# Early weight chunks, u products among output products and transpositions, and other memory for the first channel weights

## The chip, the core and the metric

The kernel runs on one core of a Trainium2 chip. The core has five engines with a queue of instructions each: TensorE (PE, with its weight loads shown as PEld), VectorE (DVE), ScalarE (ACT), GpSimd (POOL) and SyncE (SP), which here issues most of the transfers (DMA). The metric is the device time of one execution in microseconds (us); lower is better.

## The reference

Four steps are computed in turn, for 4 batches of 576 tokens with 512 features, in float32:

```
scores = 1/sqrt(D) * rot(q) @ rot(k).T ; attn = softmax(scores) ; x = heads(attn @ v)
h = gelu(x @ w_in) ; u, v = h[..., :512], h[..., 512:]
v_n = (v - mean) / sqrt(var + 1e-06) * g_ln
x = x + (u * (w_sg @ v_n + b_sg)) @ w_out           # over the tokens: w_sg is 576 x 576
u = x + (x.T @ U @ V).T                             # rank 32, over the tokens
out = u + relu(u @ w_ch1) @ w_ch2                   # 512 -> 2048 -> 512
```

All weights of the last three steps arrive as 64-bit words and are turned into float32 on the chip.

## The kernel before

**Stages.** The attention runs until about 305 us, then the gated stage for batches 0 to 3 until about 555 us, then the channel stage to the end. A float32 product is made of three products of halves (high x high, high x low, low x high); a tile's name ends in H or h for its high part and in L or l for its low part. High parts are copied by ACT, low parts are differences, made by POOL or DVE (`less`).

**The gated stage.** For a batch b it consists of these steps, each a group of products on PE and what other engines make of it:

- `v_step`: products v; gelu on ACT; the normalisation on DVE and ACT into VH, VL and, for the last 64 tokens, VT (L648, L651).
- `u_step`: products u; gelu on ACT into the tile ug.
- `s_step`: spatial products m of the matrices WSH/WSL with VH, VL (and VT); then on DVE g (L672, L673), which reads m and ug, on ACT its high part, on POOL its low part. LAST_G is the last step of g.
- `o_step`: output products w; DVE adds them to X (L691).
- `y_step`: transpositions t of X on PE (L710); ACT copies them to YH (L712), DVE makes YL (L718); of the last 64 tokens DVE makes the low part in a piece of YH (L714).
- `z_step`: products z of 512 columns from YH and YL (L728); from them ACT and DVE make Z (L731, L732).
- `h_step`: products q of V and Z; DVE adds them to X (L740). The four of a batch are q_0 to q_3.

**Weights on the side.** `other_weights` converts the four blocks of w_out, each by one ACT step (L85) and four DVE steps (L86 to L89) from a block loaded into a YH or YL tile. `first_weights` converts the first 26 blocks ("chunks", numbered from 0) of w_ch1 and w_ch2, each by an ACT step (L775) and four DVE steps (L771 to L774) out of a tile `raw` into a tile `cb`; every second chunk ends with a combine, four more DVE steps (L782 to L785), and a store of cb to memory off the core (COMBO). A generator gives out one chunk at each call of `chunk()`. A chunk's steps may be issued only behind the last marked step of DVE and the last gelu of the program so far (`issue_after` with LAST_D); a weight of w_out stands behind the last g in the same way.

**What sets the order.** In the attention and the channel stage all engines' orders are written by hand. In the gated stage only PE's is: it runs the products as the code lists them. For ACT, DVE, POOL and SP a scheduler puts the steps into an order, within what the data and `issue_after` allow. The calls for batch b are mixed with those for n = b + 1: spatial products of b, v products of n, output products of b, then u products of n among the transpositions, z and q of b.

**The channel stage.** `channel` has 12 periods of 14 ticks, each with the seven products r (L907) of w_ch1 and the seven products a of w_ch2 in a Strassen-like scheme; the operands of the second group are r1h, r1l to r7h, r7l (copies on ACT L828, differences L831). Step lists with times in ticks set every engine's order. In period 0 the high parts of the next group's weights are loaded from COMBO into YH and YL tiles (`loads`), copied by ACT to w1h, w2h (`highs`), and the low parts just used (w1l, w2l, "lows") are stored. Batch 3's transpositions, z, Z and q run in this period's first ticks. The tiles W1, W2, ROP, cb3 (`spare`) and `words` are opened in the memory that the gated stage leaves, in the order of the code.

## Time and profile before

| what | value |
|---|---|
| time, median of 3 runs (lowest to highest) | 925.42 us (924.62 to 926.44) |
| profiled execution: its own time | 929.44 us |
| its span | 927.6 us |
| mean granted clock of PE, share of full speed | 0.982 |
| busy PE, PEld | 894.3 us (96%), 809.0 us (87%) |
| busy DVE | 746.0 us (80%) |
| busy ACT, POOL | 465.3 us (50%), 400.9 us (43%) |

PE is nearly always busy over the span, so a gain has to come out of its few gaps, or out of stretches at a lower granted clock. The shares are means over three stages that differ: which engine holds PE up has to be read stage by stage.

### The profile page before, as it was taken

To read this page: it belongs to the slowest core of one execution; us is meant where nothing else is said; L and a number is where in the kernel's file an instruction comes from. 1 tells how busy PE (TensorE), PEld (TensorE's weight loads), DVE (VectorE), ACT (ScalarE), POOL (GpSimd) and SP (SyncE) were. 2 spreads that over 40 slices of the span, in tenths; PEclk is the share of its full clock that TensorE was granted. 3 is DMA by queue.
4 is the path that set the end of the run, shared out by engine and by line. 5 is a ranking of instruction groups with operands and counts; after the bars stand their busy time and mean duration, and the time that the engine had idled before them with its cause. 6 is when DMAs were issued, how large, how long until landed. Compare 5 with 4: busy or idle time off the path is not lost.

```text
span 927.6 us, 14333 instructions
## 1 busy us (share of the span) xinstructions
PE 894.3 (96%) x5279; PEld 809.0 (87%) x5279; DVE 746.0 (80%) x991; ACT 465.3 (50%) x719; POOL 400.9 (43%) x302
## 2 busy tenths in 40 slices
PE   8999999999999998798999987999999999999998
PEld 4677788878877998797899986999999999999997
DVE  6666888898998497799798886889788877897557
ACT  4555666666666554423524436455455555544232
POOL 6995787777736575142244314341011111041010
PEclk9999999999999999799899999999999999999999
DMA  6787777687662412435235238669479568737721
GB/s 189 204 183 174 208 195 192 164 214 180 164 170 57 144 46 70 145 126 192 87 124 194 87 136 275 240 230 376 166 268 353 215 213 284 249 123 266 277 98 69
DMA packets 101331, 170.36 MB, mean 184 GB/s; under 512 B 32823, under 2 KB 50509, under 8 KB 101261
## 3 DMA queue, kind: packets, MB, share of 16 engines
q1 hardware_dynamic: 100960, 169.36, 59.1%
q8 instruction: 42, 0.69, 0.3%
q14 instruction: 29, 0.23, 0.1%
q10 hardware_dynamic: 300, 0.08, 0.0%
HBM read 110.07 MB, written 41.49 MB: 163 GB/s over the span
## 4 chain that ended last, share of the span: by engine, by line
PE 62%; DVE 20%; DMA 5%; issue 4%; POOL 4%; ACT 4%; SPq 0%; DVEq 0%; POOLq 0%; ACTq 0%
PE pv L278 12%; PE st L251 7%; PE sm L209 3%; PE u L588 2%; DVE cb L774 2%; DVE cb L773 2%; DVE cb L771 1%; DVE g L672 1%; DVE g L673 1%; DVE cb L782 1%; DVE cb L772 1%; DMA YL<-combo 1%; PE a0X L907 1%; DVE MX L214 1%; PE w L588 1%
## 5 line engine op out<-in xcount | busy, mean ns | idle before, releaser
L214 DVE TENSOR_REDUCE MX<-sm 128x1 f32<-128x576 f32 (+1 forms) x160 | 117.0, 747 | 38.4 <-PE sm L209 31.9
L278 PE MATMUL pv<-pc,VV 128*65 128x288 f32 (+1 forms) x516 | 146.7, 408 | 0.0
L251 PE MATMUL st<-Q,K 65*128 65x288 f32 (+3 forms) x640 | 126.9, 321 | 3.5 <-DMA Q<-mt 2.1
L251 PEld LDWEIGHTS st<-Q,K 65*128 65x128 f32 (+3 forms) x640 | 95.6, 179 | 18.3 <-DMA Q<-mt 2.3
L254 ACT ACTIVATE pc<-st 128x576 f32<-128x576 f32 x129 | 83.1, 645 | 33.2 <-PE st L251 30.7
L278 PEld LDWEIGHTS pv<-pc,VV 128*65 128x65 f32 (+1 forms) x516 | 69.7, 137 | 29.4 <-issue 0.7
L831 POOL TENSOR_TENSOR r1l<-t,r1h 128x768 fp32r<-128x768 f32 x12 | 22.6, 1884 | 157.3 <-ACT r1h L828 141.4
L831 POOL TENSOR_TENSOR r7l<-tmp,r7h 128x768 fp32r<-128x768 f32 x12 | 25.6, 2129 | 120.4 <-ACT r7h L828 89.3
L209 PE MATMUL sm<-K,Q 128*128 128x288 f32 (+1 forms) x320 | 72.4, 316 | 1.7 <-ACT pc L254 0.6
L173 POOL TENSOR_TENSOR Q<-raw,Q 128x576 fp32r<-128x576 f32 x30 | 45.7, 1522 | 31.8 <-ACT Q L168 31.7
L209 PEld LDWEIGHTS sm<-K,Q 128*128 128x128 f32 (+1 forms) x320 | 50.4, 179 | 7.7 <-DVE MX L214 1.3
L154 POOL TENSOR_TENSOR raw<-raw,tab 128x576 f32<-128x576 f32 x31 | 50.5, 1630 | 2.5 <-DMA raw<-in_qk 2.5
L331 DVE TENSOR_TENSOR X<-stage,rb 64x576 f32<-64x576 f32 x30 | 47.5, 1586 | 1.4 <-DMA rb<-rr 1.0
L588 PE MATMUL u<-XH,setA 128*128 128x288 f32 x256 | 46.7, 299 | 1.4 <-DVE X L691 1.4
L156 POOL TENSOR_TENSOR raw<-raw 128x576 f32<-128x576 f32 x31 | 47.6, 1537 | 0.6
L155 POOL TENSOR_TENSOR raw<-raw,tab 128x576 f32<-128x576 f32 x31 | 44.4, 1431 | 0.0
L588 PEld LDWEIGHTS u<-XH,setA 128*128 128x128 f32 x256 | 38.8, 191 | 2.0 <-DVE X L691 1.7
L541 POOL TENSOR_TENSOR GL<-g,GH 128x576 fp32r<-128x576 f32 x16 | 26.4, 1653 | 32.7 <-ACT GH L674 32.7
L588 PE MATMUL v<-setA,XH 128*128 128x512 f32 x128 | 39.6, 390 | 0.0
L432 POOL TENSOR_TENSOR XL<-X,XH 128x576 fp32r<-128x576 f32 x16 | 27.1, 1715 | 23.7 <-ACT XH L429 23.7
L775 ACT ACTIVATE cb<-raw 128x512 f32<-128x512 f32 x26 | 17.5, 672 | 39.4 <-DMA raw<-in_w 27.8
L294 ACT ACTIVATE stage<-pv 65x576 f32<-65x576 f32 x31 | 20.0, 647 | 29.6 <-PE pv L278 29.6
(1149 smaller groups left out, 2508.4 us busy)
## 6 DMA issues: line engine op xcount, KB each, us to landing
raw<-in_qk SPq DMA_DIRECT2D x31, 576.0 KB
combo<-cb SPq DMA_DIRECT2D x16, 896.0 KB
YH<-combo SPq DMA_DIRECT2D x27, 512.0 KB
raw<-in_w SPq DMA_DIRECT2D x26, 512.0 KB
K<-Q SPq DMA_DIRECT2D x30, 288.0 KB
YL<-combo SPq DMA_DIRECT2D x15, 512.0 KB
u<-setA SPq DMA_DIRECT2D x16, 384.0 KB
w2l<-lows SPq DMA_DIRECT2D x12, 512.0 KB
```

Source lines behind the costliest of these rows:

```text
L154: lambda: e.tensor_tensor(raw[:, 0], raw[:, 0], tab[:, 0], ALU.mult),
L155: lambda: e.tensor_tensor(raw[:, 1], raw[:, 1], tab[:, 1], ALU.mult),
L156: lambda: e.tensor_tensor(raw[:, 0], raw[:, 0], raw[:, 1], ALU.add),
L173: nc.gpsimd.tensor_tensor(Q2[:, :S], rot, f(Q1), ALU.subtract)
L209: nc.tensor.matmul(ps[:TS[t], n, :HALF], Q1[:, t * P:t * P + TS[t]], K1[:, n * HALF:(n + 1) * HALF], start=True, stop=True)
L214: nc.vector.tensor_reduce(MXs[h % 2][:TS[t], t:t + 1], ps[:TS[t], :, :HALF], AX.XY, ALU.max)
L251: nc.tensor.matmul(ps[:kk, n, :HALF], l[:, c * P:c * P + kk], r[:, ns], start=st, stop=not st)
L254: nc.scalar.activation(h2(pc[:kk]), ps[:kk, :, :HALF], AF.Exp, scale=0.125)
L278: nc.tensor.matmul(o, l, r, start=(c == 0 and j == 0), stop=(c == NC - 1 and j == len(pr) - 1))
L331: nc.vector.tensor_tensor(X[b][rows, pr], STAGE.pop(h - 1 + a)[:D], RB[i][:, a], ALU.mult)
L588: nc.tensor.matmul(o, l, rr, start=(first and j == 0), stop=(last and j == n - 1))
L831: return e.tensor_tensor(out, a, b, ALU.subtract)
```

## The change

The code changes in six places.

- In batch 0 the gelu of the v products goes to a YL tile instead of a raw tile.
- `first_weights` is opened right behind `x_tail(0)`, and chunks 0 and 1 are called behind u_1 and u_3 of batch 0, ahead of its first spatial products. The other chunks are called at other places: for n = 1 seven as before, for n = 2 and n = 3 nine each, and chunk 25 behind m_0 of batch 3 instead of m_1.
- PE's order for n = 1: u_0 and u_1 stand ahead of the transpositions, u_2 between these and z, u_3 between z and its last product; the q products move behind the spatial products m_0 and m_1 of batch 1.
- PE's order for n = 2: u_0 stands between the transpositions and z.
- cb3 and words are opened after W1, W2 and ROP. By the addresses they now lie in the memory of the spatial weights WSH and WSL; before, they lay in memory that the output products read.
- In period 0 of the channel stage the stores of lows that stood at ticks 3.6 and 8.0 are at 6.7, and the times of the high copies change.

```diff
@@ -625,7 +625,7 @@
         nt = last - first + 1
         slot[0] = 1024 - slot[0]
         hv = ug.rearrange("p a b -> p (a b)")[:, slot[0]:slot[0] + 1024].rearrange("p (a b) -> p a b", a=2)
-        hv = (hv if b else raw_tile())[:, :nt]
+        hv = (hv if b else py.tile([P, 2, DF], F32, tag="YL", name="YL", bufs=2))[:, :nt]
         gelu(hv, ps[:pp, :nt])
         st = p2.tile([P, 2, 6], F32, tag="bst", name="bst", bufs=2)
         mv = p2.tile([P, 2, 2], F32, tag="bmv", name="bmv", bufs=2)
@@ -869,11 +869,11 @@
 
         def spare_tile():
             return pr.tile([P, 7, HF], F32, tag="cb3", name="cb3", bufs=1).rearrange("p a b -> p (a b)")
-        spare, word = {0: spare_tile()}, [word_tile()]
         seta = [t.rearrange("p a b -> p (a b)")[:, 4 * TB:] for t in SETA]
         W1 = [p3.tile([P, 5, FG], F32R, name=f"w1{x}") for x in "hl"]
         W2 = [p3.tile([P, 7, FG], F32R, name=f"w2{x}") for x in "hl"]
         ROP = {n: [pr.tile([P, 2, TB], F32R, name=f"r{n}{x}") for x in "hl"] for n in range(1, 8)}
+        spare, word = {0: spare_tile()}, [word_tile()]
 
         def wslot(c, x, j, n=1):
             if c == 0 and j >= 5:
@@ -1019,11 +1019,11 @@
                     at(o + t, lambda n=n, y=y: nc.sync.dma_start(UKEPT[p][n][:, y], f(UOP[n][y])))
             if g not in [x for _, x in ORDER[:i]] and g < NG - 1:
                 for c, j in KEPT:
-                    at(o + (0.05 if c == 0 and j < 2 else 3.6 if c == 0 else 8.0 if i == 0 else 6.0), lambda c=c, j=j: nc.sync.dma_start(LOWS[c][g][:, j], f(wslot(c, 1, j))))
+                    at(o + (0.05 if c == 0 and j < 2 else 6.7 if i == 0 else 3.6 if c == 0 else 6.0), lambda c=c, j=j: nc.sync.dma_start(LOWS[c][g][:, j], f(wslot(c, 1, j))))
             if h != g:
                 fresh = h not in [x for _, x in ORDER[:i]]
                 loads = (2.3, 4.0, 4.5, 6.5, 6.6) if i == 0 else (0.2, 0.3, 1.3, 2.4, 5.0) if i > 3 else (1.4, 1.8, 3.2, 3.5, 5.0)
-                highs = (3.85, 5.45, 6.5, 9.0, 9.4) if i == 0 else (3.85, 4.75, 6.0, 7.0, 9.4) if i == 1 else (4.1, 4.75, 6.0, 7.0, 9.4)
+                highs = (4.1, 6.2, 7.0, 9.0, 9.4) if i == 0 else (3.85, 4.75, 6.0, 7.0, 9.4) if i == 1 else (4.1, 4.75, 6.0, 7.0, 9.4)
                 tops = (15.1, 16.2) if fresh else (13.2, 14.2)
                 seconds = (11.65, 13.0, 13.6) if fresh or i == 3 else (6.1, 7.1, 8.1)
                 for c, j0, j1, load, t, lo, e in (
@@ -1114,6 +1114,9 @@
 
     spatial_weights()
     x_tail(0)
+    fw = first_weights()
+    next(fw)
+    chunk = lambda: next(fw, None)
     for t in range(NC):
         v_step(0, t)
     RB[NP - 1] = p2.tile([P, S], F32, tag="g", name="g", bufs=2)
@@ -1122,15 +1125,14 @@
             fn()
     for k0 in range(KT):
         u_step(0, k0)
+        if k0 % 2:
+            chunk()
     ow = other_weights()
     with ExitStack() as es:
         for x in LASTS:
             es.enter_context(tc.issue_after(x.ins))
         next(ow)
         x_split(1)
-    fw = first_weights()
-    next(fw)
-    chunk = lambda: next(fw, None)
     for b in range(B - 1):
         n = b + 1
         for d in range(KT):
@@ -1141,7 +1143,12 @@
                 with ExitStack() as es:
                     es.enter_context(tc.issue_after(LAST_G[0].ins))
                     next(ow, None)
-            elif d % 2:
+            if b == 1:
+                if d < 2:
+                    run(h_step, b - 1, 2 * d, 2 * d + 1)
+                if d % 2:
+                    chunk()
+            if b == 2 and d % 2 == 0:
                 chunk()
         run(v_step, n, 0, 1)
         chunk()
@@ -1162,34 +1169,41 @@
             v_step(n, 2)
             chunk()
             run(v_step, n, 3, 4)
+            if n == 3:
+                chunk()
+        if n == 1:
+            u_step(n, 0)
             chunk()
-        us = iter(range(KT))
-        if n < B - 1:
-            if n % 2:
-                u_step(n, next(us))
+            u_step(n, 1)
             run(y_step, b, 0, 2)
-            if n % 2:
-                chunk()
+            u_step(n, 2)
             run(z_step, b, *range(NC - 1))
             y_step(b, 4)
-            u_step(n, next(us))
+            u_step(n, 3)
+            z_step(b, 4)
             chunk()
+        elif n == 2:
+            run(y_step, b, 0, 2)
+            u_step(n, 0)
+            chunk()
+            run(z_step, b, *range(NC - 1))
+            y_step(b, 4)
+            u_step(n, 1)
             z_step(b, 4)
-            u_step(n, next(us))
+            u_step(n, 2)
+            chunk()
             run(h_step, b, 0, 1)
-            u_step(n, next(us))
-            chunk()
+            u_step(n, 3)
             run(h_step, b, 2, 3)
-            run(u_step, n, *us)
         else:
-            for k0 in us:
+            for k0 in range(KT):
                 u_step(n, k0)
                 if k0 % 2:
                     chunk()
     a, b = B - 2, B - 1
     for d in range(KT):
         s_step(b, d)
-        if d == 1:
+        if d == 0:
             chunk()
         if d < 2:
             y_step(a, 2 * d)
```

What this moves on the engines is not seen in the diff alone. In the rows below a number in a product's name only counts tiles; 128x512 and so on is a step's shape.

DVE at the first spatial products of batch 0, before; m_0 and m_1 are the products that g waits for, L86 to L89 the weights of w_out:

```order
L648 TENSOR_TENSOR VH<-raw,VH 64x512
L651 TENSOR_TENSOR VT<-raw,VT 64x512
L86 TENSOR_SCALAR cb<-cb 128x512
L87 TENSOR_SCALAR cb<-cb 128x512
L88 SCALAR_TENSOR_TENSOR cb<-YH,cb 128x512
L89 SCALAR_TENSOR_TENSOR cb<-YH,cb 128x512
L672 SCALAR_TENSOR_TENSOR g<-m_0_3621,small,bh 128x576
L673 TENSOR_TENSOR g<-g,ug 128x576
```

DVE at the same place after the change, from VT on; L771 to L774 are chunks, L782 is the first step of a combine:

```order
L651 TENSOR_TENSOR VT<-YL,VT 64x512
L771 TENSOR_SCALAR cb<-cb 128x2x256
L86 TENSOR_SCALAR cb<-cb 128x512
...
L774 SCALAR_TENSOR_TENSOR cb<-raw,cb 128x2x256
L89 SCALAR_TENSOR_TENSOR cb<-YH,cb 128x512
L771 TENSOR_SCALAR cb<-cb 128x2x256
L772 TENSOR_SCALAR cb<-cb 128x2x256
L773 SCALAR_TENSOR_TENSOR cb<-raw,cb 128x2x256
L774 SCALAR_TENSOR_TENSOR cb<-raw,cb 128x2x256
L672 SCALAR_TENSOR_TENSOR g<-m_0_3641,small,bh 128x576
L782 TENSOR_TENSOR cb<-cb 128x256
L673 TENSOR_TENSOR g<-g,ug 128x576
```

Chunks 0 and 1 and the first combine, twelve steps, now stand between VT and the end of the first g's; the scheduler didn't place any of them ahead of VT.

PE from the transpositions of batch 0 to the last z, before, with what stands of one u product shortened:

```order
L588 MATMUL u_0_4017<-XH,setA_71 128x288 x2
L710 MATMUL t_0_4043<-ident,X 128x128 x8
L710 MATMUL t_2_4056<-ident,X 128x128 x8
L728 MATMUL z_4077<-YH,U_76 128x512
...
L710 MATMUL z_4077<-ident,X 64x128 x4
L588 MATMUL u_1_4093<-XH,setA_70 128x288 x2
...
L588 MATMUL q_0_4161<-V_77,Z_4132 128x288 x2
L588 MATMUL q_1_4165<-V_77,Z_4132 128x288 x2
L588 MATMUL u_3_4169<-XH,setA_70 128x288 x2
```

PE after the change, from the same transpositions to the first q products:

```order
L588 MATMUL u_1_4071<-XH,setA_71 128x288 x2
L710 MATMUL t_0_4097<-ident,X 128x128 x8
L710 MATMUL t_2_4110<-ident,X 128x128 x8
L588 MATMUL u_2_4123<-XH,setA_70 128x288 x2
...
L728 MATMUL z_4149<-YH,U_76 128x512
...
L588 MATMUL m_0_4207<-WST,VT 128x288 x4
L588 MATMUL q_0_4241<-V_77,Z_4192 128x288 x2
L588 MATMUL q_1_4245<-V_77,Z_4192 128x288 x2
L588 MATMUL m_1_4257<-WS,VH 128x288 x4
```

A u product now stands between the transpositions and z, and the q products stand behind the first spatial product of batch 1. On DVE the step that they wait for, L732, stood behind one step of the next chunk; it now stands behind three:

```order
L714 TENSOR_TENSOR YH<-z_4149,YH 64x512
L771 TENSOR_SCALAR cb<-cb 128x512
L772 TENSOR_SCALAR cb<-cb 128x512
L773 SCALAR_TENSOR_TENSOR cb<-raw,cb 128x512
L732 TENSOR_TENSOR Z_4192<-z_4149,Z_4192 32x512
L774 SCALAR_TENSOR_TENSOR cb<-raw,cb 128x512
L672 SCALAR_TENSOR_TENSOR g<-m_0_4207,small,bh 128x576
L740 TENSOR_TENSOR X<-q_0_4241,X 128x576
```

The first q sum (L740) moved behind a g of batch 1.

ACT at the start of the channel stage, before; z, Z are batch 3's, r0x and r0z are sums of products r:

```order
L828 ACTIVATE r1h<-t_5853 128x768
L828 ACTIVATE w1h<-YH 128x1024
L731 ACTIVATE Z_5888<-z_5791 128x512
L828 ACTIVATE tmp<-r0z 128x768
L828 ACTIVATE w2h<-words 128x512
L828 ACTIVATE w1h<-YL 128x1024
L828 ACTIVATE r3h<-tmp 128x768
L828 ACTIVATE w1h<-YH 128x512
```

ACT at the same place after the change:

```order
L828 ACTIVATE r1h<-t_5853 128x768
L731 ACTIVATE Z_5882<-z_5791 128x512
L828 ACTIVATE tmp<-r0z 128x768
L828 ACTIVATE w1h<-YH 128x1024
L828 ACTIVATE w2h<-words 128x512
L828 ACTIVATE r3h<-tmp 128x768
L828 ACTIVATE w1h<-YL 128x1024
L828 ACTIVATE w1h<-YH 128x512
```

Z and the copy of r0z moved ahead of the first high copy, and r3h ahead of the one out of YL.

## Rows read from the trace of the kernel before

**Rows 1.** Waits of PE, 310 to 600 us: us in total, times, longest

```profile
PE t L710 <- DVE X L691: 4.1, 1, 4.1
PE z L728 <- DVE YL L718: 4.1, 4, 2.6
PE a0X L907 <- DVE X L740: 3.7, 1, 3.7
PE z L728 <- DVE YH L714: 2.1, 1, 2.1
...
PE r0x L907 <- ACT tmp L828: 1.4, 2, 1.1
```

**Rows 2.** Busy PE, PEld, DVE, ACT, POOL by stretch; granted clock, DMA share, GB/s

```profile
325.70:340.60 14.90, 14.90 (x115) 14.90 (x114) 13.78 (x14) 8.60 (x15) 11.48 (x8) 1.00 0.22 71
340.60:351.50 10.90, 10.90 (x50) 9.01 (x49) 10.76 (x13) 2.69 (x4) 6.01 (x4) 1.00 0.00 0
364.40:382.90 18.50, 10.96 (x54) 8.91 (x53) 16.26 (x30) 6.40 (x9) 3.50 (x3) 0.72 0.55 184
```

**Rows 3.** Timeline of DVE, 326 to 353: start, duration, line, output<-inputs

```profile
332.24 1.65 DVE L86 TENSOR_SCALAR cb<-cb 128x512 f32<-128x512 f32 x1
...
351.49 0.75 DVE L673 TENSOR_TENSOR g<-g,ug 128x576 f32<-128x576 f32 x1
```

**Rows 4.** Timeline of POOL, 313 to 412; in brackets the idle time before and its releaser

```profile
329.78 5.39 POOL L432 TENSOR_TENSOR XL<-X,XH 128x576 fp32r<-128x576 f32 x3 [3.42 <-ACT XH L429]
...
391.81 6.17 POOL L432 TENSOR_TENSOR XL<-X,XH 128x576 fp32r<-128x576 f32 x4 [6.28 <-ACT XH L429]
```

**Rows 5.** Timeline of DVE, 374 to 392

```profile
375.98 0.42 DVE L785 TENSOR_TENSOR cb<-cb 128x256 f32<-128x256 f32 x1
378.04 2.35 DVE L718 TENSOR_TENSOR YL<-t,YH 128x1024 fp32r<-128x1024 f32 x2 [1.63 <-ACT YH L712]
380.31 0.42 DVE L771 TENSOR_SCALAR cb<-cb 128x512 f32<-128x512 f32 x1
...
381.23 0.69 DVE L773 SCALAR_TENSOR_TENSOR cb<-raw,cb 128x512 uint32<-128x512 uint32 x1
```

**Rows 6.** Timeline of PE, 310 to 420, from u to the spatial products of batch 1

```profile
365.90 0.53 PE L588 MATMUL u<-XH,setA 128*128 128x288 f32 x2 [1.44 <-DVE X L691]
...
374.15 2.40 PE L710 MATMUL t<-ident,X 128*128 128x128 f32 x10 [4.13 <-DVE X L691]
378.06 0.80 PE L728 MATMUL z<-YH,U 128*128 128x512 f32 x1 [1.51 <-ACT YH L712]
...
393.24 0.69 PE L588 MATMUL q<-V,Z 128*128 128x288 f32 x4
393.77 0.69 PE L588 MATMUL m<-WS,VH 128*128 128x288 f32 x4
```

**Rows 7.** Timeline of PE and of DVE, 436 to 462, batch 1

```profile
437.66 0.50 PE L728 MATMUL z<-YH,U 128*128 128x512 f32 x1 [0.49 <-ACT YH L712]
440.76 0.79 PE L728 MATMUL z<-YL,U 128*128 128x512 f32 x1 [2.60 <-DVE YL L718]
...
442.28 1.23 DVE L718 TENSOR_TENSOR YL<-t,YH 128x1024 fp32r<-128x1024 f32 x1 [1.51 <-ACT YH L712]
...
460.78 0.69 PE L588 MATMUL m<-WS,VH 128*128 128x288 f32 x4
```

**Rows 8.** Timeline of all engines, 569 to 586, start of the channel stage

```profile
571.79 0.95 DVE L970 TENSOR_TENSOR tmp<-r0x,tmp 128x768 f32<-128x768 f32 x1
...
575.33 1.06 ACT L828 ACTIVATE w1h<-YL 128x1024 fp32r<-128x1024 f32 x1 [5.18 <-DMA YL<-combo]
576.29 0.83 ACT L828 ACTIVATE r3h<-tmp 128x768 fp32r<-128x768 f32 x1
...
584.06 0.95 DVE L831 TENSOR_TENSOR r6l<-tmp,r6h 128x768 fp32r<-128x768 f32 x1
...
585.41 0.51 PE L907 MATMUL a0X<-r6h,w2h 128*128 128x384 f32 x2
```

## The prediction

> **What bounds the kernel now.** I read the waits of PE first. Between 310 and 600 us PE stands idle in a few places only [rows 1]: 4.1 us for a transposition that needs X, 4.1 us in four spatial-low products z that need YL, 3.7 us ahead of a0X, 2.1 us for one z that needs YH, 1.4 us for r0x, and 1.44 us for a product u [rows 6]. Everywhere else in that stretch PE runs without a gap. So the change can gain only in those places, and the next question is who keeps PE waiting there. The busy time by stage answers it for batch 0 [rows 2]: while PE makes the spatial products m (325.7 to 340.6) DVE is busy 13.78 of 14.90 us, in the next products v 10.76 of 10.90, and around the transpositions (364.4 to 382.9) 16.26 of 18.50 while PE works 10.96. DVE is the bound of batch 0, and PE's waits there are what DVE's queue leaves over. The timeline of DVE says why the queue is long [rows 3]: a step of a kind that takes 0.42 us alone [rows 5] takes 1.65 us at 332.24, while POOL runs the differences XL [rows 4]. Last I read the start of the channel stage [rows 8].
>
> **Part 1, two chunks ahead of the first spatial products.** A chunk is four DVE steps; alone two take 0.42 and two 0.69 us, together 2.22 [rows 5]; every second chunk ends in a combine of four steps of 0.42, 1.7 us [rows 5]. DVE is idle for long before 326, but the chunks don't get there: the code lets a chunk's steps out only behind the last marked DVE step, which is VT's (L651), and the order shows them right behind it, ahead of the first g. From there DVE was full. Ahead of the last YL of batch 0 stood four chunks before, now seven (0 to 6). Three chunks and one combine are 3 x 2.22 + 1.7 = 8.4 us. One ACT step more ahead of VH and VT adds 0.6. The 1.63 us that DVE waited for YH before its two YL [rows 5] is filled by chunk 6, so 8.4 + 0.6 - 1.6 = 7.4 us: YL, which ended at 378.04 + 2.35 = 380.4, ends at 387.8.
>
> The contention needs a choice. A step that meets POOL ends about when POOL's operation ends (1.65 us for 0.42 us of work [rows 3, 5]), so it loses some 1.2 us. POOL has 12 operations in the two stretches [rows 2], as many after the change, and they already found DVE steps to hold up. I take no further loss, since the number of POOL operations doesn't change; the ends are 5 us more (four or five more meetings) and 4.7 us less (the idle DVE time of 351 to 383 takes some of it in).
>
> The Trainium skill (SBUF — State Buffer, Who interferes with whom) says that a DVE instruction with two SBUF inputs, or in a two-port mode, and a GpSimd instruction lock each other out, and that the second one waits for the whole of the first. Taken alone it would have each of the 12 early steps wait for an operation of its own; by the rows only POOL's operations are counted, not DVE's. By the one the time is 931.9, by the other 918.3; the first is the slower rival.
>
> **Part 2, u products between output products and transpositions.** In batch 0 PE now runs u_0, u_1, t_0, t_2, u_2, z, u_3. A matmul of 288 columns takes 0.133 us (four in the 0.53 from 393.24 to 393.77 [rows 6]), a u product of 24 so 3.2, two q products of eight in all 1.07. That puts 6.4 us of work where PE waited 1.44, 4.13 and 1.51 us [rows 6], and would hide all of it, and the half clock with it (0.72 granted there [rows 2]), if DVE stood still. DVE is 7.4 us later, though, so PE now waits earlier: v's first product for the place of m_0 until g is read, the third and fourth output product for gelu of v. Behind YL's end PE has four z products of 512 columns (at the same rate 0.94 us), four transpositions (0.5, ten took 2.40 at half clock [rows 6]), u_3 (3.2) and the last z (0.24): 4.9 us, so the next spatial products start at 387.8 + 4.9 = 392.7, against 393.77 before [rows 6], when two q products (1.07) were done already. Term A: -1.0 + 1.1 = **+0.1 us**, ends -4.6 and +5.
>
> **Part 3, q products behind m_0 and m_1.** They now need Z in the middle of PE's stream. DVE's Z stands behind three steps of chunk 7; that chunk's first ACT step stands behind gelu of u_3, which ends at 387.8 + 0.94 + 0.5 + 3.2 + 0.7 = 393.1, so the three can start at 393.7. POOL makes four XL meanwhile, 1.54 us each; before, they began 2.0 us ahead of m_0 (391.81 [rows 4], 393.77 [rows 6]), now so at 390.7, and last to 396.9. The three steps end about with the second, third and fourth XL [rows 3], 397.5, and Z, as long as such a step, at 398.2. PE has m_0 (28 matmuls, 3.7) done at 392.7 + 3.7 = 396.4: a new wait. Term B: **+1.8 us**, ends 0 (no contention: 393.7 + 1.5 + 0.7 lies before 396.4) and 2.6.
>
> In batch 1 u_0 moves in front of the z products. There the first z stood at 437.66, behind the transpositions, and a later one waited 2.60 us [rows 7]. PE comes 1.9 us late (A and B): 439.6, plus u_0 442.8. YL ended at 442.28 + 1.23 = 443.5 [rows 7]; ahead of it now stands one combine more (1.7) and some of the lateness (0.4): 445.6. Four z (0.94) and the transpositions (0.5) end at 447.0; u_1 to u_3, z and q are 9.6 + 0.24 + 1.07 = 10.9, so the spatial products of batch 2 start at 457.9, against 460.78 [rows 7]: 2.9 early, from 1.9 late. Term C: **-4.8 us**, ends -3 and -6.5.
>
> By the end of batch 1 both kernels have done 16 chunks. In batch 2 and 3 PE had no wait but the z for YH (2.1 us [rows 1]); there I take DVE as 2.1 us early, since its last combine ahead of g is now done sooner but its q sums later, while PE is 2.9 early, so the wait grows. Chunk 25 moves from behind m_1 to behind m_0, with as much work ahead of that YH as before. Term D: **+0.8 us**, ends -0.9 and +0.9.
>
> **Part 4, first weights.** The buffers cb3 and words now lie in WS, last read by m, not in memory that the output products read to the end; their loads can start some 14 us earlier. PE's first channel product waited little for them, so this alone gives little: it moves ACT and DVE steps forward that PE's short waits there hang on (r0x for copies on ACT, 1.4 us in two [rows 1]). I take 1.1 of that. The new times do more. Before, a load into YL was issued behind five stores of lows, ACT waited 5.18 us for it, and r3h, which needs nothing of it, stood behind on ACT until 576.29 [rows 8]. Its input was done at 571.79 + 0.95 = 572.74. Now r3h stands ahead of that step and the stores behind the loads: r3h 3.5 us earlier, and with it r3l, X, a0X. PE then meets DVE again: r6l began at 584.06 and now begins at 580.6, ends 581.5, and the second a0X product, at 585.41 before [rows 8], can start then: 3.9 us. Term E: -3.9 - 1.1 = **-5.0 us**, ends -2 and -6.6.
>
> Edits without a price: hv of batch 0 in YL instead of raw (as many buffers; the loads of output weights 1 and 3 now wait for VL and VT, until 326 and 328, and are wanted at 344); weight 2's first step waits for the store of the first pair (issued about 346; DVE comes to that step at 351 and the store has 5 us until then, about what a load into YL took on ACT's account [rows 8]; 1 to 2 us if that cover is gone); the stores of lows at 6.7, before the 9.4 at which their places are written.
>
> **The sum.** 0.1 + 1.8 - 4.8 + 0.8 - 5.0 = -7.1 us. The profiled execution took 929.44 (span 927.6 and 1.8 around it), 4.0 above the median of the runs, 925.42; I apply the difference to the median: **918.3 us**.
>
> **Rivals.** First, the waits of batch 0 simply go: DVE absorbs the early chunks in its idle time. Then A is -7.1 for the three waits and -2.9 for work at half clock (half of the 2.40 us of ten transpositions, and some 0.21 for each of eight z), B is 0, and the sum is -19.0: 906.4. For it speaks PE's new cover, against it DVE at 99% in v. Chance 0.10. Second, slower: the 12 early steps each meet a POOL operation at about 1.65 us, 19.8 instead of 6.2; A becomes +13.7 and the time 931.9. It decides from some 0.6 us per step above the time alone. The rows of XL speak for it, POOL's count of 12 against it. Chance 0.08. Third, the channel's start is held by DVE whatever arrives earlier: E is -0.5 and the time 922.8; the short PE waits there speak for it, the 5.18 us wait against it. Chance 0.14.
>
> **How the numbers follow.** The forecast has 0.68. Its terms' ends, not all at once, give 912 to 924.5; the third rival lies inside, and of the two others half a chance of the first is taken in at the lower end: 911.5 to 924.5. About 0.2% is what a measurement here can tell from no change: below 923.6 lie 0.63 of the forecast, 0.10 of the first rival and 0.08 of the third, 0.81; within 0.2% 0.05 and 0.05, 0.10; above 0.09, nearly all the second.
>
> **What would show it.** Right: the last g of batch 0 some 6 us later than 351.49, YL of batch 0 ending near 388, a wait of q for Z, a z wait in batch 1 below 1 us, no load wait ahead of r3h, and the second a0X product 5 us sooner against the first channel product. Wrong: g of batch 0 not later (then 906.4), steps of 1.65 us all along chunks 0 and 1 (931.9), a0X still waiting over 3 us (923).

## The result and the profile after

The changed kernel takes 913.64 us (median of 4 runs, 912.03 to 914.42), the kernel before 925.02 beside it (4 runs, 924.23 to 926.44): a ratio of 0.9873, 95% interval 0.9855 to 0.9892. That is 11.4 us less (10.0 to 13.4 by the interval of the ratio), where 7.1 were forecast. The time lies in the range of 911.5 to 924.5; the sign was right, the size too small. The profiled execution of the changed kernel took 912.03 us, its span 910.2, at a mean granted clock of 0.996 (0.982 before).

**The same waits after.** PE's waits between 305 and 600 us in the changed kernel (us in total, times, longest), to be laid beside [rows 1]:

```profile
PE q L588 <- DVE Z L732: 2.5, 1, 2.5
PE u L588 <- DVE X L691: 1.9, 1, 1.9
PE z L728 <- DVE YL L718: 1.5, 1, 1.5
PE w L588 <- ACT WOH L573: 1.1, 1, 1.1
PE a0X L907 <- DVE X L991: 1.0, 1, 1.0
PE w L588 <- POOL GL L541: 0.9, 1, 0.9
PE w L588 <- ACT ug L579: 0.9, 1, 0.9
PE w L588 <- POOL WOL L541: 0.8, 1, 0.8
PE z L728 <- DVE YH L714: 0.7, 1, 0.7
```

The wait of the transpositions for X (4.1 us) and the wait for a0X on the sums of q (3.7) are gone or 0.2, the two z waits for YL in batch 1 (3.1 us) are gone (the 1.5 that is left is batch 0's), the one for YH of batch 2 has fallen from 2.1 to 0.7. New are the wait of q for Z, 2.5 us, three waits of the products w in batch 0 (for WOH, ug and WOL, 2.8 in all) and one of w in batch 3 (for GL, 0.9, at 525.71), which stood in nobody's way before.

**Where the time went, by stage.** Both traces are read from the first product v, since what lies ahead of it differs from run to run and isn't touched by the change (it starts at 299.47 us in the trace before, at 295.88 in the one after). Each stage runs up to the named start on PE's timeline; all are worked out as differences of such starts.

| stage, up to the start of | before | after | difference | forecast |
|---|---|---|---|---|
| m, batch 1 | 94.30 | 92.84 | -1.5 | -1.0 |
| v, batch 2 (the q products now lie in here) | 14.93 | 18.75 | +3.8 | +2.9 |
| m, batch 2 (term C) | 52.08 | 44.60 | -7.5 | -4.8 |
| m, batch 3 | 51.47 | 51.48 | 0.0 | with D |
| first r0x (term D) | 40.04 | 37.59 | -2.5 | +0.8 |
| first r1x (term E) | 43.52 | 36.96 | -6.6 | -5.0 |
| end | 331.79 | 332.10 | +0.3 | 0 |

The differences add up to 13.8 us. The medians give 11.4: one trace of each kernel stands for its median to about 2 us here, and a single stage without any edit differs by up to 1.7 us between traces (the last row: 331.2 to 332.9 over the runs below; the second row: 18.75, 20.28 and 20.27 in the changed kernel, chunk25_back and n2_back, which differ in nothing up to there). Terms are therefore read to about 1.5 us.

**DVE in batch 0.** The timeline of DVE in the changed kernel, with the early chunks (L771 to L774) among output weight 0 (L86 to L89), and at YL and Z:

```profile
323.17 0.69 DVE L651 TENSOR_TENSOR VT<-YL,VT 64x512 fp32r<-64x512 f32 x1
...
326.09 1.93 DVE L88 SCALAR_TENSOR_TENSOR cb<-YH,cb 128x512 uint32<-128x512 uint32 x1
327.94 1.92 DVE L774 SCALAR_TENSOR_TENSOR cb<-raw,cb 128x512 uint32<-128x512 uint32 x1
329.78 1.91 DVE L89 SCALAR_TENSOR_TENSOR cb<-YH,cb 128x512 uint32<-128x512 uint32 x1
331.62 1.65 DVE L771 TENSOR_SCALAR cb<-cb 128x512 f32<-128x512 f32 x1
333.30 1.39 DVE L772 TENSOR_SCALAR cb<-cb 128x512 uint32<-128x512 uint32 x1
...
352.44 0.75 DVE L673 TENSOR_TENSOR g<-g,ug 128x576 f32<-128x576 f32 x1
...
381.64 2.35 DVE L718 TENSOR_TENSOR YL<-t,YH 128x1024 fp32r<-128x1024 f32 x2
...
392.59 1.77 DVE L773 SCALAR_TENSOR_TENSOR cb<-raw,cb 128x512 uint32<-128x512 uint32 x1
394.38 0.69 DVE L732 TENSOR_TENSOR Z<-z,Z 32x512 fp32r<-32x512 f32 x1
```

POOL at the same time (timeline):

```profile
325.63 7.35 POOL L432 TENSOR_TENSOR XL<-X,XH 128x576 fp32r<-128x576 f32 x4 [3.41 <-ACT XH L429]
332.94 1.47 POOL L541 TENSOR_TENSOR WOL<-cb,WOH 128x512 fp32r<-128x512 f32 x1
...
387.85 5.95 POOL L432 TENSOR_TENSOR XL<-X,XH 128x576 fp32r<-128x576 f32 x4
```

Five steps take 1.39 to 1.93 us instead of 0.42 to 0.69, all of them beside POOL's four XL and the low part of output weight 0 (WOL); three of them are steps of the early chunks, two are steps of output weight 0. The chunks did not all pay for POOL: they stood where output weights had stood in the kernel before [rows 3]. Counted from VT to the end of the last g, nine DVE steps take 1.3 us or more in the changed kernel, and eight in the kernel before. YL of batch 0 ends at 383.99, 88.1 us behind the first v, against 80.9 before [rows 5]: 7.2 us later, where 7.4 were forecast. At Z the chunk step ahead of it takes 1.77 us during the second four XL.

### The profile page after: what moved, and what is told of

The parts are those of the page before. It is cut to its first block, busy times and chain, and to the rows that moved or that the text cites. A ratio compares the mean times of both kernels' runs of the same rounds, so it can differ in the third digit from the quotient of the medians.

```text
span 910.2 us, 14331 instructions
## 1 busy us (share of the span) xinstructions
PE 885.3 (97%) x5279; PEld 802.9 (88%) x5279; DVE 738.8 (81%) x991; ACT 464.7 (51%) x719; POOL 401.9 (44%) x302
## 4 chain that ended last, share of the span: by engine, by line
PE 65%; DVE 21%; DMA 4%; ACT 4%; issue 4%; POOL 2%; SPq 0%; DVEq 0%; POOLq 0%; ACTq 0%
PE pv L278 12%; PE st L251 8%; PE sm L209 4%; DVE cb L773 2%; PE v L588 2%; PE w L588 1%; PE u L588 1%; DVE cb L774 1%; DVE cb L771 1%; DVE MX L214 1%; PE m L588 1%; DVE cb L772 1%; PE a2X L907 1%; PE r2x L907 1%; PE a4X L907 1%
## 5 line engine op out<-in xcount | busy, mean ns | idle before, releaser
L258 ACT ACTIVATE pt<-st 64x576 f32<-64x576 f32 x31 | 19.9, 643 | 27.7 <-PE st L251 27.6
```

## The experiments

All times are ratios to the kernel before on the same chip, with their 95% interval. The changed kernel's is 0.9873.

| run | ratio | interval | us against the kernel before, about |
|---|---|---|---|
| times_only | 0.9961 | 0.9943 to 0.9978 | -3.6 |
| memory_only | 0.9969 | 0.9956 to 0.9982 | -2.9 |
| chunks_only | 1.0025 | 1.0007 to 1.0044 | +2.3 |
| order_only | 0.9885 | 0.9864 to 0.9906 | -10.6 |
| order_channel | 0.9826 | 0.9802 to 0.9849 | -16.1 |
| free_chunks | 0.9822 | 0.9801 to 0.9843 | -16.5 |
| q_back | 0.9911 | 0.9891 to 0.9931 | -8.2 |
| chunk25_back | 0.9853 | 0.9833 to 0.9873 | -13.6 |
| z_first | 0.9873 | 0.9845 to 0.9901 | -11.8 |
| n2_back | 0.9920 | 0.9896 to 0.9945 | -7.4 |
| free_best | 0.9811 | 0.9785 to 0.9837 | -17.5 |
| free_earlier | 0.9759 | 0.9736 to 0.9783 | -22.3 |

(The last column is the ratio less one times 926 us.)

### One part at a time

**times_only**: the kernel before, with

```diff
-  3.6 if c == 0 else 8.0 if i == 0 else 6.0          # stores of lows
+  6.7 if i == 0 else 3.6 if c == 0 else 6.0
-  highs = (3.85, 5.45, 6.5, 9.0, 9.4) if i == 0
+  highs = (4.1, 6.2, 7.0, 9.0, 9.4) if i == 0
```

> The kernel before with one edit: in period 0 of the channel stage the stores of lows at tick 6.7 and the new times of the high copies. Theory (r3h no longer waits behind the copy out of YL, which waits for its load): the wait of 5.18 us on ACT falls off PE's path, the second a0X product comes some 4 us sooner against the first r product, 921 us (range 919.5 to 922.5). Rival (DVE holds the channel's start whatever arrives earlier): 924.5 us, and PE still waits over 3 us for a0X.

ACT at the start of the channel stage in times_only (timeline):

```profile
571.49 0.85 ACT L828 ACTIVATE r3h<-tmp 128x768 fp32r<-128x768 f32 x1 [3.14 <-DVE tmp L970]
572.24 1.04 ACT L828 ACTIVATE w1h<-YL 128x1024 fp32r<-128x1024 f32 x1
```

r3h now waits for its input alone, and the copy out of YL behind it for nothing. The stage up to the first r1x is 39.4 us, 4.1 shorter, and the time 3.6 us less: the theory's 3.9. The first a0X product comes 3.3 us sooner behind the first r0x, the second 1.1 us sooner behind the first; the rival (DVE holds the start) is out.

**memory_only**: the kernel before, with

```diff
-  spare, word = {0: spare_tile()}, [word_tile()]
   ...
   ROP = {n: [...] for n in range(1, 8)}
+  spare, word = {0: spare_tile()}, [word_tile()]
```

> The kernel before with one edit: cb3 and words opened behind W1, W2 and ROP, so that they lie in the memory of the spatial weights. Theory: the first loads of the channel stage start some 14 us earlier, but little waited for them: 924 us (923 to 925), the wait of ACT for the load into YL stays near 5 us. Rival (the earlier loads alone also bring the load into YL forward): 921 us, that wait under 2 us.

ACT in memory_only (timeline):

```profile
568.88 1.06 ACT L828 ACTIVATE w1h<-YL 128x1024 fp32r<-128x1024 f32 x1 [5.41 <-DMA YL<-combo]
569.84 0.83 ACT L828 ACTIVATE r3h<-tmp 128x768 fp32r<-128x768 f32 x1
```

The wait for the load into YL stays (5.41 us; 5.18 in [rows 8]), as the theory says, and r3h still stands behind it. The gain, 2.9 us by the time and 2.0 in the stage, is larger than the 1.1 taken for it: r0x waits 0.6 us for ACT in all instead of 1.4 [rows 1]; where the rest comes from isn't settled.

**chunks_only**: the changed kernel with PE's old order in batches 1 and 2 and the old channel start. For n = 1:

```diff
 u_step(n, 0)
 chunk()
-u_step(n, 1)
 run(y_step, b, 0, 2)
-u_step(n, 2)
 run(z_step, b, *range(NC - 1))
 y_step(b, 4)
-u_step(n, 3)
+u_step(n, 1)
 z_step(b, 4)
 chunk()
+u_step(n, 2)
+run(h_step, b, 0, 1)
+u_step(n, 3)
+run(h_step, b, 2, 3)
```

> The changed kernel with PE's old order in batches 1 and 2 (u, transpositions, z and q as before) and the old channel start; chunks 0 and 1 early and the others' new places stay. Theory: YL of batch 0 ends 7.4 us later as in the changed kernel, and nothing on PE covers it: the spatial products of batch 1 start 7 us later than in the kernel before, measured from the first product v; 2 to 4 us come back behind batch 1, where fewer chunks stand ahead of YL; 929 us (926 to 932). Rival (DVE takes the early chunks into its idle time): within 2 us of the kernel before.

The spatial products of batch 1 start 103.0 us behind the first v, 8.7 later than before; up to the end of the gated stage 2.7 us come back in batch 1 (49.4 instead of 52.1) and 1.9 behind the spatial products of batch 3 (38.1 instead of 40.0). The time is 2.3 us above the kernel before. So the chunks' new places alone make the kernel slower, and not by the 8.7 us, since stages behind get shorter. The rival (DVE takes them in) is out by the 8.7 us; by the time alone (2.3 us, interval 0.6 to 4.1) it couldn't be told from a change of 2 us.

**order_only**: the kernel before with PE's new order, chunks and channel start as before.

In short, not as lines of code:

```diff
-  (u_0, t, chunk, z, u_1, chunk, last z, u_2, q_0 q_1, u_3, chunk, q_2 q_3 for n = 1)
+  (u_0, u_1, t, chunk, u_2, z, u_3, chunk, last z, chunk; q behind m_0 and m_1)
-  (t, z, u_0, chunk, last z, u_1, ... for n = 2)
+  (t, u_0, z, u_1, chunk, last z, u_2, ...)
```

> The kernel before with PE's new order of u, transpositions, z and q alone; chunks and channel start as before. Theory: the u products cover the waits for X and YL of batch 0 (7 us) and most of the z waits of batch 1 (4 us) with the half clock behind them; q behind m_0 waits for Z up to 2.5 us: 916 us (912 to 919). Rival (the waits only move to z and q, since DVE is the bound of batch 0): 922 us or more.

The order alone brings 10.6 us, nearly what the whole change does. The spatial products of batch 1 start 84.7 us behind the first v (94.3 before), the wait of t for X is 1.0 us, and q waits 2.9 us for Z. The rival (the waits only move) is out.

**order_channel**: order_only and the two channel edits.

> PE's new order and both edits of the channel start, the chunks as in the kernel before. Theory (terms add): 10.7 us of the order alone and 3.6 and 2.9 us of the two channel edits, 17 us off the kernel before: 908.5 us, 6 us under the changed kernel, so that the early chunks and the new places cost that much. Rival (the chunks' new places pay for themselves in batches 1 to 3, 2.7 and 2.4 us there): within 2 us of the changed kernel.

The terms add: 10.6, 3.6 and 2.9 make 17.1, and 16.1 were measured. This kernel has none of the chunk edits, and it is below the changed kernel by 4.3 us by the ratios, but only by 1.4 in the two traces, measured from the first v to the end. So the chunk edits together cost something between these two; neither the theory's 6 us nor the rival's 2 us or less is settled. By stage the spatial products of batch 1 start 85.6 us behind the first v, against 92.8 in the changed kernel: 7.2 us for the chunks' places in batch 0 (the two early ones, and six calls behind them instead of seven). Of these, 2.1 come back up to the spatial products of batch 2 (46.7 against 44.6), 1.5 up to the first r0x (39.1 against 37.6), and 1.5 in the stage with the q products (20.3 against 18.8), where the granted clock differs (0.92 against 1.00) behind the same wait of 2.5 us for Z.

### What of the changed kernel can be taken back

**q_back**: the q products ahead of the spatial products again.

```diff
-            u_step(n, 3)
             z_step(b, 4)
             chunk()
+            u_step(n, 3)
+            run(h_step, b, *range(KT))
...
-                if d < 2:
-                    run(h_step, b - 1, 2 * d, 2 * d + 1)
```

> The changed kernel with the four q products of batch 0 ahead of the spatial products of batch 1 again, behind u_3, and the last z ahead of u_3. Theory: the 2.5 us that q waited for Z are replaced by a wait of the last z for YH of some 1.6 us; the products v of batch 2 start 0 to 1.5 us sooner, the time is within 1.5 us of the changed kernel, so that the move itself brought nothing. Rival (the move hides Z): 2 us or more above the changed kernel.

The theory fell: it is 3.5 us above the changed kernel. The wait of the last z for YH came about as expected (1.4 us) and Z was in time, but a longer wait came elsewhere. The largest wait of PE in q_back, which the changed kernel hasn't, and DVE's timeline there:

```profile
PE m L588 <- DVE X L740: 4.6, 1, 4.6
```

```profile
390.05 0.69 DVE L732 TENSOR_TENSOR Z<-z,Z 32x512 fp32r<-32x512 f32 x1
...
391.91 1.53 DVE L782 TENSOR_TENSOR cb<-cb 128x256 f32<-128x256 f32 x1
...
394.90 1.62 DVE L784 TENSOR_TENSOR cb<-cb 128x256 f32<-128x256 f32 x1
396.55 1.42 DVE L740 TENSOR_TENSOR X<-q,X 128x576 f32<-128x576 f32 x2
```

Four q products in a row take all four of PE's result tiles (the kernel's pool `ps2` has four), and m_0 has to wait until DVE has added the first of them to X; the sums stand behind three steps of a combine at 1.5 us each. Behind m_0 and m_1 the q products need two tiles at a time. The move is worth its place, for a reason that the prediction didn't name.

**z_first**: chunk 7 behind m_0 of batch 1, so that Z has nothing ahead of it on DVE.

```diff
             u_step(n, 3)
             z_step(b, 4)
-            chunk()
...
                     run(h_step, b - 1, 2 * d, 2 * d + 1)
+                if d == 0:
+                    chunk()
```

> The changed kernel with chunk 7 called behind m_0 of batch 1, so that Z stands on DVE behind YH and not behind three steps of that chunk. Theory (the new wait of q is those three steps, each held up by a difference XL on POOL): the wait of 2.5 us for Z falls under 0.8, the products v of batch 2 start 1.7 to 2.5 us sooner, the time is 2 us under the changed kernel. Rival (Z is late because of z and YH, not of the chunk): the wait stays over 1.5 us and the time within 0.7 us.

The wait of q for Z is gone: term B's mechanism, three steps of chunk 7 held up by XL, is shown. The stretch from the spatial products of batch 1 to the products v of batch 2 is 16.0 us instead of 18.8. But the spatial products of batch 1 start 1.9 us later than in the changed kernel, so that the products v of batch 2 start only 0.9 us sooner, and the time is the same. In the trace, what took the gain is the stretch from the z products to the end of the last z, first in z_first, then in the changed kernel (columns as in [rows 2]):

```profile
381.20:390.65 9.45, 7.87 (x37) 6.48 (x38) 3.81 (x5) 4.72 (x9) 2.90 (x4) 0.82 0.44 137
```

```profile
381.00:388.72 7.72, 6.23 (x40) 5.17 (x39) 3.64 (x4) 4.34 (x9) 2.26 (x3) 1.00 0.49 154
```

It runs at a granted clock of 0.82 instead of 1.00 and takes 1.7 us more, with the same wait for YL in it (1.5 us). That the edit brought this isn't shown: the moved chunk lies behind the stretch, and the traces differ ahead of it too. In the changed kernel u_0 and u_1, just ahead of the transpositions, took 8.0 us at a granted clock of 0.79; in z_first they took 6.5 at 1.00, and t then waited 1.0 us for X, which it doesn't in the changed kernel. In free_best below, which moves the same chunk, the stage behind is 16.0 us as well, and the z products run at 1.00. Why the time of z_first is the same stays open.

**n2_back**: PE's old order for n = 2.

```diff
             run(y_step, b, 0, 2)
-            u_step(n, 0)
             chunk()
             run(z_step, b, *range(NC - 1))
             y_step(b, 4)
-            u_step(n, 1)
+            u_step(n, 0)
             z_step(b, 4)
-            u_step(n, 2)
+            u_step(n, 1)
...
```

> The changed kernel with PE's old order in batch 2's u products: no u product between the transpositions and z of batch 1. Theory (YL of batch 1 is ready sooner in the changed kernel because one chunk less stands between the products v and it, so that u_0 has little left to cover): the stretch from the products v of batch 2 to the spatial products of batch 2 grows by 2 to 3.5 us over the 44.6 us of the changed kernel. Rival (u_0 covers all of the difference): it grows to the 52.1 us of the kernel before, 7.5 us.

The stretch from the products v to the spatial products of batch 2 is 49.4 us, 4.8 more than in the changed kernel and 2.7 less than in the kernel before: neither the theory's 2 to 3.5 nor the rival's 7.5. The time is 4.4 us above the changed kernel. With chunks_only (2.7 of the 7.5) it divides the stage: u_0 ahead of z is worth 4.8 us, the chunks' new places 2.7. order_only, with u_0 ahead of z and the old places, agrees: 46.9 us, 5.2 less than the kernel before.

**chunk25_back**: chunk 25 behind m_1 (`if d == 1`) as before.

> The changed kernel with chunk 25 behind m_1 of batch 3 as before. Theory (its earlier place is what freed YH of batch 2, and with it the half clock of the output products): the stretch from the spatial products of batch 3 to the first product r is 2 us longer, the time 2 us above the changed kernel. Rival (the number of chunks ahead decides, not this one's place): no difference in that stretch above 0.5 us.

The stretch is 37.2 us (37.6 in the changed kernel), the time no worse; the rival holds. The wait of z for YH is 1.5 us here and 0.7 in the changed kernel, but the changed kernel has 0.9 us of waiting for GL ahead of it, which isn't here: chunk 25's place only divides the waiting another way.

### The early chunks at another place

DVE is nearly idle while PE makes the u products of batch 0, just ahead of VT. **free_chunks** lets the two chunks out there:

```diff
     for t in range(NC):
         v_step(0, t)
+        if t > 2:
+            chunk()
...
     for k0 in range(KT):
         u_step(0, k0)
-        if k0 % 2:
-            chunk()
...
-                for x in LAST_D:
+                for x in LAST_D if j > 1 else LAST_D[1:]:
```

> The changed kernel, but chunks 0 and 1 are called among the products v of batch 0 and don't stand behind VT: on DVE their steps lie in the stretch in which it is busy only 3.42 of 12.50 us. Theory (the early chunks were dear because they stood ahead of the first g): YL of batch 0 ends 6 to 7 us sooner than in the changed kernel, PE's waits in the output products and for YL go, the spatial products of batch 1 start 5 to 7 us sooner, 5 to 7 us less than the changed kernel in all (about 908 us where the kernel before takes 925). Rival (the four XL of POOL then hold up other steps as long): less than 2 us gained.

4.7 us are gained by the time, but only 1.5 in the trace, and the mechanism isn't the expected one: the last g still ends 57.0 us behind the first v (57.3 in the changed kernel, 52.8 before), and YL 86.6 (88.1). DVE's timeline in free_chunks:

```profile
322.68 1.40 DVE L782 TENSOR_TENSOR cb<-cb 128x256 f32<-128x256 f32 x1
...
327.77 1.55 DVE L86 TENSOR_SCALAR cb<-cb 128x512 f32<-128x512 f32 x1
...
332.76 1.80 DVE L89 SCALAR_TENSOR_TENSOR cb<-YH,cb 128x512 uint32<-128x512 uint32 x1
```

The combine (L782) met POOL's differences VL and stood ahead of VH and VT; output weight 0 came 2.4 us later than in the changed kernel and met the XL with all four steps. Work of 6.2 us was taken out of the stretch, and DVE's last g came only 0.3 us sooner: other steps were held up instead. For g the rival was right.

**free_best** puts chunk 6 behind YL and chunk 7 behind m_0 besides:

```diff
             u_step(n, 0)
-            chunk()
             u_step(n, 1)
             run(y_step, b, 0, 2)
+            chunk()
             u_step(n, 2)
```

> The changed kernel with three edits: chunks 0 and 1 among the products v of batch 0 (as free_chunks), chunk 6 behind YL of batch 0 instead of ahead of it, chunk 7 behind m_0 of batch 1 so that Z has nothing ahead of it. Theory (what PE still waits for in batch 0 is the chunks that stand ahead of YL and Z): the spatial products of batch 1 start 86 us after the first product v (91.3 in free_chunks, 92.8 in the changed kernel), q waits under 1 us for Z, the later stages keep the changed kernel's lengths; 6 to 8 us less than free_chunks: ratio to the kernel before 0.975 (904 where the kernel before takes 927). Rival (the two moved chunks then hold up g or the next YL as long): within 3 us of free_chunks, ratio 0.979 or more.

The wait for Z is gone and YL ends 85.3 us behind the first v, but the spatial products of batch 1 start at 90.0, not 86: g is as late as in free_chunks. It is 5.7 us below the changed kernel, both by the time and in the trace. Against free_chunks the theory's 6 to 8 us did not come: 1.0 us by the ratios, whose intervals overlap, and 4.2 in the traces. By the ratio (0.9811) the rival was right.

**free_earlier** lets the two chunks out behind the second and the fourth product v (`if t in (1, 3)`).

> free_best with chunks 0 and 1 called one and two products v earlier (behind the second and the fourth of batch 0). In free_best the first combine stood ahead of VH and VT on DVE, met POOL's differences VL (1.40 us for steps of 0.42), and the steps of output weight 0 behind it then met POOL's XL (1.55 to 1.80 us each). Theory (the combine's place is what kept g as late as in the changed kernel): PE's wait of 0.9 us for VH goes, the last g of batch 0 ends 53 to 55 us after the first product v (57.1 in free_best, 52.8 in the kernel before), 2 to 4 us less than free_best: ratio 0.978. Rival (whatever stands there, DVE meets as many operations of POOL): the last g stays within 1 us of 57.1 and the time within 1.5 us of free_best.

DVE's timeline in free_earlier:

```profile
319.46 0.42 DVE L782 TENSOR_TENSOR cb<-cb 128x256 f32<-128x256 f32 x1
...
325.87 0.43 DVE L86 TENSOR_SCALAR cb<-cb 128x512 f32<-128x512 f32 x1 [0.43 <-ACT cb L85]
...
327.52 1.80 DVE L89 SCALAR_TENSOR_TENSOR cb<-YH,cb 128x512 uint32<-128x512 uint32 x1
...
350.18 0.75 DVE L673 TENSOR_TENSOR g<-g,ug 128x576 f32<-128x576 f32 x1
```

The combine takes 0.42 us a step, three of output weight 0's steps are through ahead of the XL, the last g ends 55.2 us behind the first v, the wait for VH is gone, and the spatial products of batch 1 start at 88.1. At 904.69 us (ratio 0.9759) it is the fastest kernel of the study. The expected 0.978 lies in its interval. Against free_best it is 4.8 us less by the ratios and 0.6 in the traces: 1.9 are gained up to the spatial products of batch 1, and the stretch behind the first r1x, which the edit doesn't touch, is 1.0 longer. The mechanism (the combine out of the way, the last g sooner) is shown; its worth is known only as 1.9 us in its stage.

## Why the prediction was right, and where not

**Batch 0, terms A and B: right, by the steps given.** YL was 7.2 us late (7.4 forecast), the spatial products of batch 1 started 1.5 us sooner (1.0), q waited 2.5 us for Z (1.8) behind three steps held up by XL, as z_first shows by taking them away. The u products cover the waits, as order_only shows. Of the places named for PE's earlier wait, the one for gelu of v came (ug, 0.9 us), the one of v's first product did not (v starts 41.17 us behind the first v, 41.12 before), and 1.9 us stood at WOH and WOL, the parts of an output weight, which the prediction did not name. The first rival (the waits of batch 0 simply go) failed at the point named: the last g ended 4.5 us later (6 forecast). What was not seen is why the q products belong behind m_0: not as a price, but because four in a row would wait for their own sums (q_back).

**The contention: the choice was right.** The Trainium skill (SBUF — State Buffer, Who interferes with whom) says that a DVE instruction with two SBUF inputs, or in a two-port mode, and a GpSimd instruction lock each other out, and that the second waits for the whole of the first. The trace agrees: of the five steps held up, the three of 0.69 us end 0.55 us behind the end of an operation of POOL and the two of 0.42 us end 0.3 us behind one, if the four XL share their 7.35 us evenly. The slow reading of it, each of the 12 early steps at about 1.65 us, did not come: three of the 12 met one of POOL's operations, and two steps of output weight 0 met two others. That POOL's operations count and not DVE's steps held in the other direction too: free_chunks took the twelve steps away, and the four of output weight 0 met POOL in their place. In these traces the loss went with POOL's operations, as the forecast took it: nine steps of DVE held up to the last g, eight before.

**Batch 1, term C: the mechanism right, one sign wrong and one size too large.** -7.5 us against -4.8. u_0 ahead of z was taken for more than it is worth: without the combine the term's own sum ends at 456.2, which is -6.5, and u_0 is worth 4.8 (n2_back) to 5.2 (order_only). The step that failed is "ahead of it now stands one combine more (1.7)": the chunks' places took 2.3 to 2.7 us off the stage instead of adding 1.7, and the two errors partly cancel. DVE at batch 1's YL in the kernel before, where a whole chunk stands ahead of the normalisation and YL:

```profile
434.19 0.43 DVE L771 TENSOR_SCALAR cb<-cb 128x512 f32<-128x512 f32 x1 [0.71 <-ACT cb L775]
...
436.05 0.69 DVE L774 SCALAR_TENSOR_TENSOR cb<-raw,cb 128x512 uint32<-128x512 uint32 x1
436.65 1.28 DVE L634 BATCH_NORM_STATS2 bst<-ug 128x6 f32<-128x512 f32 x2
```

and in the changed kernel, where the normalisation follows on a combine and no chunk is left:

```profile
432.38 0.42 DVE L785 TENSOR_TENSOR cb<-cb 128x256 f32<-128x256 f32 x1
432.72 1.28 DVE L634 BATCH_NORM_STATS2 bst<-ug 128x6 f32<-128x512 f32 x2
...
438.48 1.23 DVE L718 TENSOR_TENSOR YL<-t,YH 128x1024 fp32r<-128x1024 f32 x1 [1.03 <-ACT YH L712]
```

The change drops the chunk call behind the last products v for n = 2 (the new code has it for n = 3 alone). The list of the change has this wrong: the code calls six chunks for n = 1, eight for n = 2 and nine for n = 3, where seven, nine and nine stood before. DVE's normalisation holds up ACT's, and this the second YH, which the second YL waits for; ACT at that place, before and after:

```profile
439.82 1.52 ACT L641 ACTIVATE ug<-ug,bmv,brs 128x512 f32<-128x512 f32 x2 [2.22 <-DVE bmv L635]
```

```profile
436.02 1.51 ACT L641 ACTIVATE ug<-ug,bmv,brs 128x512 f32<-128x512 f32 x2
```

The second YL ends 5.7 us behind the first transposition (434.03) instead of 8.3 (435.25, [rows 7]). The combine was counted in, the chunk that went was overlooked: 2.6 us sooner, not 1.7 later. That this one call did it is read from the timelines; the runs show it only for all new places of the chunks together. z then waits for nothing, and PE's stretch from the transpositions to the spatial products runs at full clock (busy PE, PEld, DVE, ACT, POOL, granted clock, DMA share, GB/s; first before, then after):

```profile
435.25:460.78 25.53, 21.97 (x135) 19.44 (x134) 19.89 (x37) 14.27 (x22) 5.67 (x7) 0.87 0.43 135
```

```profile
434.03:452.07 18.04, 18.04 (x134) 17.59 (x133) 13.02 (x22) 13.90 (x22) 6.23 (x8) 1.00 0.28 93
```

**Batch 2 and 3, term D: wrong sign.** -2.5 us against +0.8. The step that failed is "so the wait grows". The wait of z for YH fell from 2.1 to 0.7 us, but 0.9 us of waiting for GL came ahead of it, so that the stretch from the first w to that z hardly changed (6.98 us, 7.10 before). 0.6 us were gained in the spatial products ahead of it (18.8 us, 19.4 before), and 1.5 us are the clock behind the wait, again before and after:

```profile
538.79:548.64 9.85, 9.85 (x61) 9.80 (x62) 8.15 (x10) 2.40 (x4) 0.00 (x0) 0.83 0.00 0
```

```profile
529.36:537.67 8.31, 8.31 (x61) 8.27 (x62) 8.21 (x10) 3.96 (x7) 1.48 (x1) 1.00 0.00 0
```

The same 61 matmuls take 9.85 or 8.31 us. Term D had no place for the clock. It was argued with chunk 25, whose place makes no difference to the stage (chunk25_back); the chunks' other places do (chunks_only has -1.9 here, order_only +0.4). What decides the clock stays open. The wait goes with it only in part: of the fourteen traces, the four with these matmuls at a lower clock (the kernel before, times_only, memory_only, order_only) have waits of 2.04 to 2.07 us for YH ahead of them, nine others have 0.7 to 1.5, but order_channel waits 2.02 us, and its 61 matmuls run at 1.00.

**Channel start, term E: right, with one size too small.** -6.6 us against -5.0. r3h and the loads were worth what was said (3.6 to 4.1 against 3.9), the first weights' memory 2.0 to 2.9 instead of 1.1; the second a0X product came 6.8 us sooner behind the first channel product, where 5 were named. ACT and then PE in the changed kernel, where the load into YL is not waited for and the second a0X product comes 5.5 us behind the first (6.6 before):

```profile
559.40 0.85 ACT L828 ACTIVATE r3h<-tmp 128x768 fp32r<-128x768 f32 x1 [3.01 <-DVE tmp L970]
560.15 1.04 ACT L828 ACTIVATE w1h<-YL 128x1024 fp32r<-128x1024 f32 x1
```

```profile
567.43 0.59 PE L907 MATMUL a0X<-r6h,w2h 128*128 128x384 f32 x2 [1.03 <-DVE X L991]
```

**The sum** came out 4.3 us too small against the medians, 6.7 against the two traces, since the three misses (C by 2.7, D by 3.3, E by 1.6) all lie on the same side; A and B were 0.5 us too good. The forecast as a case held, none of the rivals did. That the time still lies in the range, 2.1 us above its lower end, owes something to the range's width and not to the terms C and D, whose reasons for the chunks' part were wrong.

## What to carry to other kernels

Price a bundle of edits one by one: here the order of the products on PE and the channel start made the gain, and the chunk edits as a whole cost 1.4 us (traces) to 4.3 us (ratios), since the places in batch 0, the two chunks ahead of its spatial products first of all, cost 7 us there and the places behind gave only a part back. With those chunks in DVE's empty stretch and two others moved, the kernel is 6.2 us (ratios) or 4.9 us (traces) below the one without any of the chunk edits. When side work is handed out at new places, list for every later stage which call went as well as which came: here the chunks that no longer stood ahead of a step turned the sign of a part of a term. And work taken out of a stretch in which two engines hold each other up needn't shorten it by its own length; here it counted how many operations of the other engine the queue still met.

## What of the hardware was not expected

The same 61 matmuls took 9.85 us at a granted clock of 0.83 and 8.3 at 1.00, in two kernels (the kernel before and order_channel) with a wait of 2.0 to 2.1 us ahead of them; a wait's price was so once 1.7 times the wait, and once the wait alone. The wait of q for Z shows it too: in six traces it lasts 2.5 us, and in three of them (chunk25_back, n2_back, order_channel) the next spatial products run at the lower level, 1.2 GHz, for a while (granted clock 0.92 over the stage), in the other three at full clock. The code of chunk25_back and n2_back up to there is that of the changed kernel, and DVE and ACT make the same steps in the same order. PE in the changed kernel, then in chunk25_back:

```profile
395.13 0.80 PE L588 MATMUL q<-V,Z 128*128 128x288 f32 x4 [2.52 <-DVE Z L732]
395.76 0.69 PE L588 MATMUL m<-WS,VH 128*128 128x288 f32 x4
```

```profile
395.09 0.93 PE L588 MATMUL q<-V,Z 128*128 128x288 f32 x4 [2.53 <-DVE Z L732]
395.82 1.16 PE L588 MATMUL m<-WS,VH 128*128 128x288 f32 x4
```

The stage takes 18.75 us in the one and 20.28 in the other. So one trace of a kernel does not tell what such a wait costs.

DVE steps of 128 x 256 elements with 0.42 us of work took 1.40 to 1.62 us beside POOL, as long as steps of 128 x 512 with 0.42 us of work (1.39 to 1.65); steps with 0.69 us of work took 1.77 to 1.93. In the lines shown a step beside POOL took about 1.0 to 1.25 us more than alone, whatever its own size.
